# Top-k attention with mixture of depths: half loads ahead of the scores, and the last keys' product in the tiling of the values

## The chip, the cores and the metric

The kernel runs on one core of one Trainium2 chip. The metric is the device time of one execution in microseconds (us). Five engines with queues of their own work beside each other: PE (TensorE, matrix products; its weight loads are listed as PEld), DVE (VectorE), ACT (ScalarE), POOL (GpSimd) and SP (SyncE, which issues most DMAs). Inputs are in HBM, tiles in SBUF (128 partitions), results of PE in PSUM.

## The reference

```python
scores = scale * np.matmul(q, k.transpose(0, 1, 3, 2))      # 8 batches, 8 heads, 576 tokens, 64 wide
kth = np.partition(scores, -top_k, axis=-1)[..., -top_k:-top_k + 1]   # top_k = 32
scores = np.where(scores >= kth, scores, -1000000000.0)
attn = softmax(scores)
x = concat_heads(np.matmul(attn, v))                        # (8, 576, 512)
...
gate = x @ w_gate                                           # per token
top_idx = the 128 tokens of the batch with the largest gate
out = x
out[top_idx] = x[top_idx] + sigmoid(gate) * (relu(x[top_idx] @ w1) @ w2)   # w1 512 x 1024
```

All in float32.

## The kernel before

**Tiles.** The 576 tokens of a batch are 4 tiles of 128 and one of 64 (J = 4, R = 64). A unit is one tile of queries with two heads; for the tile of 64 it holds four heads, two of them on the upper 64 partitions. So a batch has 4 x 4 + 2 = 18 units, and the 8 batches 144. In what follows, "step i" of a batch is the i-th of its 18.

**The pipeline.** One loop (L1094) runs over steps n and has five units in flight. In step n, in the order of the program: the scores of unit n-4 are turned, masked and exponentiated (`weigh`, L1123); the mask of unit n-3 is made (L1126); the scores of unit n+1 are multiplied (`multiply`, L1131); a piece of the next batch's k or q is turned (the half loads, L1135); the values of unit n-4 are multiplied (`values`, L1142); DVE looks for a lower bound of the 32nd largest score of unit n (`bound_of`) and for the 32nd largest itself of unit n-2 (`kth_of`); ACT and POOL prepare unit n-1 for it (`what_is_below`: ACT writes sides, POOL writes y in two halves and a short third instruction). Behind that comes a piece of the MLP of the batch before (`mixtures`, L1179). Every engine's order is that of the program (`InOrder`, L37); only `late`, `vector_late` and `pool_late` hold a few instructions back to fixed places.

**The turned scores on PE.** `turn` (L482) and `turn_last` (L491) make nine pairs: a transpose of 128 x 128 scores (float32, against ident), and a product that adds a large negative number where the mask less is set (bf16). Eight pairs go to the tile ptr, the ninth, with the last 64 keys of both heads, to the upper columns of av. ACT's exponentials then write pT (from ptr) and last (from av).

**The scores on PE.** `multiply` (L355) takes 64 rows of kT and qT (one head's width) by up to 128 queries, so it runs in PE's tiling of 64 rows by 128 columns (64\*128 in the profile). Its result goes to the one buffer of the tile ps, 288 columns in each of four banks. The upper columns of two of the banks are the room for half loads (`halves`, L1134). `keep` (L372) copies the scores to SBUF on ACT (sc).

**The half loads.** `Rows` (L214) fetches k and q of the next batch by rows on SP's queue and turns them to kT and qT: in 16 pieces of two 128 x 128 transposes (`turn`, tiling 128\*128), and two pieces for the last 64 tokens (`turn_last`, 64 rows, tiling 64\*128). When the second piece of a buffer is turned, the next rows are fetched (L283). Each piece is a pair of functions (`parts`, L297): the first turns on PE, the second copies to kT or qT on ACT. `loads_at` (L994) gives one piece to most steps, two to steps 14 and 15; steps 1 and 3 get the pieces of the last 64 tokens, steps 2 and 16 none. In the last batch there are none, and in the first one they begin at step 2.

**The values on PE.** `values` (L503) multiplies pT by v for queries 0 to 63 and 64 to 127 apart, into the lower and upper 64 partitions of av (128 rows by 64 columns, 128\*64). The product of the last 64 keys follows (last by vpair, two heads at once): for a tile of 128 queries one product of 128 queries (128\*128), for the tile of 64 queries two of 64 (128\*64). `keep_values` (L535) copies av to xs on ACT.

The lines of the loop around the change (L1128 to L1142):

```python
        if is_unit(n + 1):
            b, t, g = units[n + 1]
            ps = room_for_scores()
            multiply(t, g, *qkv[b][0:2], ps)
            b, i = divmod(n, per_batch)
            loads = list(islice(loading, first_loads[i] if b == 0 else loads_at[i]))
            halves = [ps[:, a, :, HALF : HALF + P] for a in range(2)]
            for load, half in zip(loads, halves):
                load[0](half)
            scs[n + 1] = keep(ps, n == -1)
            for load, half in zip(loads, halves):
                load[1](half)
```

On DVE, besides the search: prod (`dot`, L940, the gate: x times w_gate, added up), junk (ranks of the gates), pick, low and, in step 0, one half of a mask (less). The float32 product of a transpose or of other operands shows in the profile as several instructions where PE takes more than one pass.

Of the kernel before, what the change touches and what calls it, by code (L numbers as in the profile page):

```python
# [31 lines left out]
J = 4  # L32
# [16 lines left out]
def kernel(  # L49
# [12 lines left out]
    P = nc.NUM_PARTITIONS  # L62
# [6 lines left out]
    R = S - JP  # L69
    HALF = S // 2  # L70
    DE = D + 1
# [96 lines left out]
    def load_weights():  # L168
        sp.dma_start(
            out=wg, in_=dataclasses.replace(moe_w_gate, ap=[[0, P], [1, HD]])  # L170
        )
        sp.dma_start(out=w1, in_=moe_w1.rearrange("(c p) f -> p c f", p=P))
        sp.dma_start(out=w2, in_=moe_w2.rearrange("(c p) n -> p c n", p=P))
# [13 lines left out]
    def flush():  # L187
        while late:
            late.pop(0)()
# [15 lines left out]
    def room_for_qkv(b):  # L205

        kT = kqpool.tile([P, NHP, R + S], FP32, name="kT")  # L210
        qT = kqpool.tile([P, NHP, S], FP32, name="qT")
        return kT, qT, vbufs[b % 2]

    class Rows:  # L214
# [70 lines left out]
        def keep(self, i, tr, c0=0, c1=J, copy=None):  # L285
            copy = copy or act.copy
            if i % 2 == 0:
                to = self.kT[:, i // 2, R + c0 * P : R + c1 * P]
            else:
                to = self.qT[:, i // 2, c0 * P : c1 * P]  # L290
            to = to.rearrange("p (c i) -> p c i", i=P)
            if i % 2 == 0:
                copy(out=to, in_=tr)
            else:
                act.mul(out=to, in_=tr, mul=SMALLER)
# [15 lines left out]
    def turn_pair(rows, hp, copy=None):  # L311
        tr = ps_tr.tile([P, 2, J, P], FP32, name="ptr")
        for w in range(2):
            rows.turn(2 * hp + w, tr[:, w, :, :])
        for w in range(2):
            rows.keep(2 * hp + w, tr[:, w, :, :], copy=copy)
# [8 lines left out]
    def load_v(vb, vs):  # L325
        vt, vpair = vs
        v_rows = vb[:, JP:S, :].rearrange("h p d -> p h d")
        for hh in range(2):
            sp.dma_start(
                out=vpair[hh * R : (hh + 1) * R, :, hh, 0:D], in_=v_rows[:, hh::2, :]  # L330
            )
        for h in range(H):
            sp.dma_start(
                out=vt[:, h, :, 0:D],
                in_=vb[h, 0:JP, :].rearrange("(p j) d -> p j d", j=J),
            )
# [5 lines left out]
    def heads_of(t, g):  # L342

        if t == J:
            return [[(4 * g + i, 0), (4 * g + 2 + i, R)] for i in range(2)]
        return [[(2 * g + i, 0)] for i in range(2)]  # L350

    def room_for_scores():
        return ps_sc.tile([P, 2, 2, 512], FP32, name="ps")

    def multiply(t, g, kT, qT, ps):  # L355

        n = R if t == J else P  # L360
        for u in range(2):
            for i, heads in enumerate(heads_of(t, g)):
                at = u * HALF + (0 if i else R)
                d = slice(i * D, (i + 1) * D)
                for h, r in heads:
                    pe.matmul(
                        ps[r : r + n, i, u, 0:HALF],
                        qT[d, h // 2, t * P : t * P + n],
                        kT[d, h // 2, at : at + HALF],
                    )  # L370
# [106 lines left out]
    def room_to_turn():  # L477
        return ps_tr.tile([P, 2, J, P], FP32, name="ptr"), ps_av.tile(
            [P, 512], FP32, name="av"
        )  # L480
# [22 lines left out]
    def values(t, g, pT, last, av, vs):  # L503

        vt, vpair = vs
        n = R if t == J else P
        for i, heads in enumerate(heads_of(t, g)):
            for c in range(J):
                for r in (0, R):
                    h = heads[-1 if r else 0][0]
                    pe.matmul(
                        av[r : r + R, i * DE : (i + 1) * DE],
                        pT[:, i, c, r : r + R],
                        vt[:, h, c, :],  # L520
                        start=(c == 0 and i == 0),
                        stop=False,
                        skip_group_check=True,
                    )
        for h, r in heads_of(t, g)[0]:
            pe.matmul(
                av[r : r + n, 0 : 2 * DE],
                last[:, r : r + n],
                vpair[:, h // 2, :, :].rearrange("p h e -> p (h e)"),
                start=False,  # L530
                stop=True,
                skip_group_check=True,
            )
# [9 lines left out]
    def normalise(b, t, xs):  # L543
        n = R if t == J else P
        den = sums[0:n, b * NT + t, :]
        divide(n, xs, of_batch[b][0][0:n, t, :], den)
# [407 lines left out]
    def gates(b, t):  # L954
        dot_tile(t, *of_batch[b])
# [51 lines left out]
    for b in range(B - 1):  # L1007
        n = (b + 1) * per_batch + mix_at_of.get(b, mix_at)[6]
# [3 lines left out]
    qkv = {0: room_for_qkv(0)}  # L1012
# [18 lines left out]
    scs, bounds, ys, next8s, masks = {}, {}, {}, {}, {}  # L1031

    def is_unit(n):
        return 0 <= n < N
# [59 lines left out]
    for n in range(-1, N):  # L1094
        b, i = divmod(n, per_batch)
        if i == 0 and 0 <= b < B - 1:
            qkv[b + 1] = room_for_qkv(b + 1)
            loading = chain(
                loading, Rows(k[b + 1], q[b + 1], *qkv[b + 1][0:2]).parts()
            )  # L1100
        if 0 < n + 1 < NHP:
            turn_pair(first_rows, n + 1)
        if n == 1:
            load_v(v[0], qkv[0][2])
        if n == NHP:
            load_weights()


        gating = normalised
        if inverting is not None:  # L1110
            normalised = inverting[0:2]
            vector_late.insert(0, lambda a=inverting: normalise(*a))
            inverting = None
        else:
            normalised = None
        if gating is not None:
            vector_late.append(lambda a=gating: gates(*a))

        if is_unit(n - 4):
            tr, av = room_to_turn()
            pT, last, exp = weigh(scs.pop(n - 4), tr, av, masks.pop(n - 4))  # L1123
            exp()
        if is_unit(n - 3):
            mask_of(n - 3, (act, None) if n in scatter_steps else None)  # L1126
        flush()
        if is_unit(n + 1):  # L1128
            b, t, g = units[n + 1]
            ps = room_for_scores()  # L1130
            multiply(t, g, *qkv[b][0:2], ps)  # L1131
            b, i = divmod(n, per_batch)
            loads = list(islice(loading, first_loads[i] if b == 0 else loads_at[i]))
            halves = [ps[:, a, :, HALF : HALF + P] for a in range(2)]  # L1134
            for load, half in zip(loads, halves):  # L1135
                load[0](half)
            scs[n + 1] = keep(ps, n == -1)
            for load, half in zip(loads, halves):
                load[1](half)
        if is_unit(n - 4):  # L1140
            b4, t4, g4 = units[n - 4]
            values(t4, g4, pT, last, av, qkv[b4][2])  # L1142
            if n in place_steps:
                values_bank[0] = av
                next(mixtures[place_steps[n]])
            if g4 == 0:
                xs = xpool.tile([P, H, DE], FP32, name="xs")
                if t4 == 0:
                    x = xpool.tile([P, NT, HD], FP32, name="x")
                    pg = gates_of[b4 % 2]  # L1150
                    of_batch[b4] = x, pg
            keep_values(t4, g4, av, xs)
            if g4 == groups(t4) - 1:
                inverting = b4, t4, xs
                n4 = R if t4 == J else P
                keep_sums(n4, xs, sums[0:n4, b4 * NT + t4, :])
            while kept:
                kept.pop(0)()


        if is_unit(n):
            bound_of(n)
        flush_vector()
        flush_pool()
        if is_unit(n - 2):
            kth_of(n - 2)
        while after_kth:
            after_kth.pop(0)()


        if is_unit(n - 1):
            what_is_below(n - 1)

        if gating is not None:
            b, t = gating
            if t == J:
                store(out[b], of_batch[b][0])
                mixtures[b] = mixture(float(b * S), of_batch[b][1], ranks[:, b, :])
        for b in mix_steps.get(n, ()):  # L1179
            next(mixtures[b], None)  # L1180
        b, i = divmod(n, per_batch)
        if i == v_at and 0 <= b < B - 1:
            load_v(v[b + 1], qkv[b + 1][2])
# [220 lines left out]
```

## Time and profile before

| | us |
|---|---|
| three runs: median, lowest, highest | 833.55, 833.13, 837.34 |
| the profiled execution | 837.12 |
| its span (first to last instruction) | 834.8 |
| PE busy in the span | 792.3 |
| DVE busy | 795.3 |
| ACT busy | 735.2 |
| POOL busy | 728.4 |

The granted clock of PE is full from 60 us on. In the timeline, a row gives start, duration, engine, operation, out<-in, tiling (PE only), shape and count; in brackets, how long the engine was idle before it and what ended that. PE's products are pipelined, so the distance from start to start is what one costs, not its duration. The table by windows gives the window, its length, and for each engine the busy time in it (and the number of instructions): PE, PEld, DVE, ACT, POOL, then the granted clock, the share of DMA and GB/s. A row of waits reads: who waited, for whom; us in total, times, longest. Where a tile's view is shown, the three numbers behind the count are the shortest, median and longest duration in ns.

### The profile page before, as it was taken

The numbers are of one execution on the slowest core, as the hardware profiler recorded it, in microseconds if no ns is written. First come the engines' busy times: TensorE is split into PE (matmuls) and PEld (weight loads), VectorE is DVE, ScalarE is ACT, GpSimd is POOL, SyncE is SP. The second block draws the span as 40 slices with busy tenths as digits, with TensorE's granted clock in tenths as the row PEclk, the third lists the DMA queues.
The fourth block names the chain that finished last, engine by engine and source line by source line (L and its number), as shares of the span: only waits on it lengthen the run. The fifth ranks groups of instructions, "written<-read, shape, count | busy, mean of one in ns | idle before, by whom it ended". The sixth has DMA issues, their size and how long they took to land. (4 is left out here: it accounts for less than half of the span.)

```text
span 834.8 us, 27764 instructions
## 1 busy us (share of the span) xinstructions
PE 792.3 (95%) x9887; PEld 613.0 (73%) x9887; DVE 795.3 (95%) x4651; ACT 735.2 (88%) x1557; POOL 728.4 (87%) x722
## 2 busy tenths in 40 slices
PE   6899889998999999999999999999999999999977
PEld 5677667766887778777787777877788778867844
DVE  7899999999999999999999999999999999899960
ACT  4799999999999999999999999999999999879831
POOL 4699999999999899999999999999999999989831
PEclk9699999999999999999999999999999999999999
DMA  7931112321151221511233221412215102101011
GB/s 171 284 78 36 32 65 54 78 52 27 59 101 24 53 46 54 111 40 39 78 63 67 48 47 59 98 27 53 40 59 111 27 2 77 23 2 27 3 70 29
DMA packets 122130, 50.35 MB, mean 60 GB/s; under 512 B 116416, under 2 KB 116416, under 8 KB 120960
## 3 DMA queue, kind: packets, MB, share of 16 engines
q1 hardware_dynamic: 118672, 43.91, 22.0%
q0 software_dynamic: 1728, 4.20, 2.7%
q8 instruction: 80, 1.31, 0.7%
q14 instruction: 66, 0.54, 0.3%
q10 hardware_dynamic: 1584, 0.39, 0.2%
HBM read 36.93 MB, written 11.55 MB: 58 GB/s over the span
## 5 line engine op out<-in xcount | busy, mean ns | idle before, releaser
L45 POOL TENSOR_TENSOR y<-sc,sides 128x576 f32<-128x576 f32 x288 | 366.3, 1294 | 65.4 <-ACT sides L45 62.5
L45 DVE MAX8 cand<-sc 128x8 f32<-128x82 f32 (+1 forms) x2016 | 313.8, 227 | 2.2 <-ACT sc L45 2.2
L45 POOL TENSOR_SCALAR less<-sc,next 128x576 bf16<-128x576 f32 x135 | 233.5, 1729 | 2.8 <-DVE next L45 1.9
L45 ACT ACTIVATE sides<-sc,bound 128x576 bf16<-128x576 f32 x288 | 222.0, 780 | 0.0
L45 PE MATMUL ptr<-out_of_reach,less 128*128 128x128 bf16 x1136 | 205.4, 220 | 14.1 <-POOL less L45 13.9
L45 PE MATMUL ptr<-ident,sc 128*128 128x128 f32 x1136 | 215.1, 280 | 0.0
L45 DVE MAX8 next<-y 128x8 f32<-128x584 f32 x288 | 204.5, 752 | 2.8 <-POOL y L45 2.6
L45 PE MATMUL ps<-kT,qT 64*128 64x288 f32 (+1 forms) x1280 | 181.0, 431 | 7.6 <-ACT qT L45 5.8
L45 ACT ACTIVATE pT<-ptr 128x1024 f32<-128x1024 f32 x142 | 145.2, 1022 | 38.6 <-PE ptr L45 34.8
L45 PEld LDWEIGHTS ptr<-ident,sc 128*128 128x128 f32 x1136 | 161.4, 142 | 22.4 <-PE av L45 8.7
L45 PEld LDWEIGHTS av<-v,pT 128*64 128x64 f32 x4544 | 144.1, 137 | 39.4 <-ACT last L45 24.2
L45 PE MATMUL av<-v,pT 128*64 128x65 f32 x4544 | 163.8, 224 | 8.2 <-ACT last L45 8.2
L45 ACT COPY sc<-ps 128x1152 f32<-128x1152 f32 (+1 forms) x144 | 161.1, 1119 | 9.6 <-PE ps L45 9.0
L45 PEld LDWEIGHTS <-less 128*128 128x128 bf16 x1296 | 134.1, 104 | 33.5 <-POOL less L45 19.5
L45 PEld LDWEIGHTS ps<-kT,qT 64*128 64x128 f32 (+1 forms) x1280 | 97.8, 177 | 46.6 <-issue 22.0
L45 ACT ACTIVATE less<-sc,next 128x576 bf16<-128x576 f32 x143 | 111.2, 777 | 6.4 <-DVE next L45 6.0
L45 DVE MATCH_REPLACE8 cand<-best,cand 128x21 f32<-128x21 f32 (+1 forms) x576 | 98.9, 179 | 0.0
L45 DVE MAX8 best<-cand 128x8 f32<-128x21 f32 (+1 forms) x576 | 90.2, 189 | 0.0
L45 PE MATMUL av<-vpair,last 128*128 128x130 f32 (+1 forms) x314 | 68.1, 317 | 0.0
L45 PE MATMUL h_ps<-xeT,w 128*128 128x128 f32 x464 | 61.6, 277 | 0.0
L45 ACT ACTIVATION_READ_ACCUMULATOR sides<-sc,bound 128x1 f32 x288 | 58.0, 201 | 0.0
L45 PEld LDWEIGHTS h_ps<-xeT,w 128*128 128x128 f32 x464 | 56.0, 192 | 2.1 <-issue 1.2
(133 smaller groups left out, 905.8 us busy)
## 6 DMA issues: line engine op xcount, KB each, us to landing
v<-in_v_dram SPq DMA_DIRECT2D x64, 128.0 KB, 3.7
out_dram<-x SPq DMA_DIRECT2D x8, 1024.0 KB, 4.0
rows<-in_k_dram SPq DMA_DIRECT2D x56, 128.0 KB, 3.0
rows<-in_q_dram SPq DMA_DIRECT2D x56, 128.0 KB, 3.0
w<-in_moe_w_dram SPq DMA_DIRECT2D x2, 2048.0 KB
gate_row<-row_dram SPq DMA_DIRECT2D x7, 288.0 KB, 4.5
w<-in_k_dram SPq DMA_DIRECT2D x8, 128.0 KB, 3.2
last<-in_k_dram SPq DMA_DIRECT2D x8, 128.0 KB, 3.6
```

Source lines behind the costliest of these rows:

```text
L45: return lambda *a, **kw: self._tc.keep_in_program_order(fn(*a, **kw))
```

## The change

In a step, the half loads are turned on PE ahead of the scores, and ACT copies them to kT or qT ahead of the copy of the scores. And the product of the last keys is always made as two products of 64 queries.

```diff
@@ values @@
         vt, vpair = vs
-        n = R if t == J else P
         for i, heads in enumerate(heads_of(t, g)):
...
-        for h, r in heads_of(t, g)[0]:
+        for r in (0, R):
+            h = heads_of(t, g)[0][-1 if r else 0][0]
             pe.matmul(
-                av[r : r + n, 0 : 2 * DE],
-                last[:, r : r + n],
+                av[r : r + R, 0 : 2 * DE],
+                last[:, r : r + R],
                 vpair[:, h // 2, :, :].rearrange("p h e -> p (h e)"),
                 start=False,
                 stop=True,
@@ the loop @@
             ps = room_for_scores()
-            multiply(t, g, *qkv[b][0:2], ps)
+            kT, qT = qkv[b][0:2]
             b, i = divmod(n, per_batch)
             loads = list(islice(loading, first_loads[i] if b == 0 else loads_at[i]))
             halves = [ps[:, a, :, HALF : HALF + P] for a in range(2)]
             for load, half in zip(loads, halves):
                 load[0](half)
-            scs[n + 1] = keep(ps, n == -1)
+            multiply(t, g, kT, qT, ps)
             for load, half in zip(loads, halves):
                 load[1](half)
+            scs[n + 1] = keep(ps, n == -1)
```

## Prediction

> **What bounds the kernel now.** I read the busy shares first, then the same for one batch in the middle, then the waits of that part, and last the timeline of single steps; the chain that ended last covers only the closing 0.1% of this span and says nothing here.
>
> ```profile
> PE 792.3 (95%) x9887; PEld 613.0 (73%) x9887; DVE 795.3 (95%) x4651; ACT 735.2 (88%) x1557; POOL 728.4 (87%) x722
> ...
> 418.00:516.00 98.00, 97.00 (x1233) 75.43 (x1231) 97.89 (x576) 92.00 (x198) 90.66 (x87) 1.00 0.27 59
> ...
> ACT pT L45 <- PE ptr L45: 21.7, 58, 0.6
> PE av L45 <- ACT last L45: 4.0, 8, 0.6
> ...
> PE ptr L45 <- POOL less L45: 12.6, 22, 1.2
> ...
> L45 DVE CUSTOM_DVE_ANT_0 prod<-x,wg x40: 672/1128/1752, 57.5 to 804.7; 128x512 f32<-128x512 f32 x32, 64x512 f32<-64x512 f32 x8
> ```
>
> The second line is the batch from 418 to 516 us: PE is busy for 97.00 of 98 us and DVE for 97.89. Both look like the bound, and the change touches only PE and the order on ACT, so everything hangs on which of the two it is. The next two lines are from 220 to 690 us: in 58 steps the exponential of the turned scores (pT) starts when PE has finished, and PE itself waits 8 times, 4.0 us. The line on POOL less is from 60 to 780 us; from 220 us on it is gone, so those 22 waits of PE lie early, and there PE is not the bound. The last line says why DVE's 97.89 is not a fixed amount of work: the same instruction prod takes 0.67 to 1.75 us.
>
> ```profile
> 442.17 2.52 POOL L45 TENSOR_TENSOR y<-sc,sides 128x576 f32<-128x576 f32 x2
> 443.15 1.02 ACT L45 ACTIVATE pT<-ptr 128x1024 f32<-128x1024 f32 x1 [0.37 <-PE ptr L45]
> 443.22 1.24 PE L45 MATMUL ps<-kT,qT 64*128 64x288 f32 x8
> 444.04 1.20 DVE L45 CUSTOM_DVE_ANT_0 prod<-x,wg 128x512 f32<-128x512 f32 x1
> 444.39 0.44 PE L45 MATMUL ps<-ident,rows 128*128 128x128 f32 x2
> 444.76 1.16 PE L45 MATMUL av<-v,pT 128*64 128x65 f32 x32
> 445.84 0.49 PE L45 MATMUL av<-vpair,last 128*128 128x130 f32 x2
> 446.17 1.05 PE L45 MATMUL h_ps<-xeT,w 128*128 128x128 f32 x8
> ```
>
> This is one step. On PE it goes, start to start: turned scores 441.58 to 443.22 (1.64 us), scores 1.17, half load 0.37, values 1.08, last keys 0.33, MLP product 0.89; the sum, 5.48, is the distance of this pT (443.15) from the next (448.64). PE works through without a gap and ACT waits 0.37 us for it: PE sets the pace. DVE's prod starts at 444.04, while POOL's two y run to 444.69, and ends 0.55 us after them: of its 1.20 us some 0.53 are standing behind POOL. From 225 to 690 us the prod (24, mean 1199 ns, least 672), less (4, 1213 against 501), pick (5, 582 against 286) and low (4, 377 against 174) stand like this for 12.6 + 2.8 + 1.5 + 0.8 = 17.7 us, 3.7 us in a batch. POOL's y wait for ACT's sides, ACT for PE. So DVE is full, but part of its time is a wait whose end PE sets.
>
> In each batch of 18 steps this holds from step 4 to the pT of step 0 of the next batch. In between ACT paces five steps (pT from 492.78 to 519.35, 5.31 us each, no wait), and PE's waits for "last" lie there (0.57 and 0.43 us); a faster PE only waits longer there.
>
> **Edit 1, half loads before the scores.** At every switch of PE's tiling the next weights are not loaded early: the weight loads stand idle for 0.16 us ahead of the scores, 0.39 ahead of the half load and 0.17 ahead of the values (440 to 446 us). Before, a step with a half load of 128 rows goes 128\*128, 64\*128 (scores), 128\*128 (half load), 128\*64 (values). After, the half load joins the turned scores, and one excursion is gone. The same step without a half load is in the last batch:
>
> ```profile
> 710.48 0.22 PE L45 MATMUL av<-out_of_reach,less 128*128 128x128 bf16 x1
> 710.62 1.24 PE L45 MATMUL ps<-kT,qT 64*128 64x288 f32 x8
> 711.81 1.15 PE L45 MATMUL av<-v,pT 128*64 128x65 f32 x32
> ```
>
> Before, from the last less product of the turned scores to the values: 0.15 + 1.17 + 0.37 = 1.69 us. After: less to the first transpose 0.06 (as inside the turned scores), transpose to transpose 0.11 (the four of xe follow each other so: 500.73 to 501.17), the last transpose to the next tiling 0.20 (0.20 from the half load's second transpose to the values, at 444.56 and 444.76), scores to values 1.19 (710.62 to 711.81). Sum 1.56 us. At the trace's full resolution the two sums are 1.689 and 1.548: **0.14 us saved in a step**. What the trace lacks is the switch from this transpose to the scores' tiling; nearest are that 0.20 and the 0.15 from a bf16 product to the scores. With 0.15 the saving is 0.19. At the dear end the gap after the scores, 0.33 us, is put there too, and the saving is 0.01. I take 0.20: it is from the same kind of instruction. With two half loads in a step the saving is the same, since their extra transposes cost 0.11 us in either place. The loads of the last 64 tokens (64 rows, the scores' own tiling) had no switch before (scores 1.07 us); they may gain one and cost up to 0.1 us, but both lie in the ACT-paced steps 1 and 3, where PE has its 0.57 and 0.43 us of wait for cover.
>
> **How many steps.** Half loads of 128 rows lie in steps 0, 4 to 15 and 17. Of these, 13 are in the PE-paced run of a batch (4 to 15 and 17). Such runs are whole in batches 3 to 6; in batch 2 it starts at step 6 (11 steps); batches 0 and 1 are paced by POOL, ACT and DVE (the 22 waits for less), and the last batch loads nothing. 11 + 4 x 13 = 63 steps x 0.14 = **8.8 us**.
>
> **The order on ACT.** The copy of the half load (0.38 us, 0.55 for two) goes ahead of the copy of the scores. Nothing is added, and xs and sides come after both as before. The half load's copy now waits for the scores, as the scores' copy before waited for the half load; that end comes earlier by 0.15 us. The scores are ready for DVE 0.4 to 0.55 us later. In batches 3 to 6 they lie ready 1.7 to 3.5 us before their first MAX8, so that is hidden. It isn't in the start: DVE waits for the scores at 24.96 (1.37 us) and at 36.01 (0.79 us), and there it costs 0.2 to 0.3 us each. I set **0.5 us**; the end for no cover at all is 98 steps (14 in each of 7 batches) x 0.39 = 38 us, which would need DVE to wait for sc, and after 60 us it never does. The scores' buffer is released at the same time, since the two copies end together. The turns also fetch the next rows on SP's queue: their order there is the same, each fetch some 1.2 us earlier, and rows land 3 us after the issue but are used two steps, 11 us, later; PE has no wait for them now.
>
> **Edit 2, the last keys in the values' tiling.** Steps that hold the last tokens do it like this already:
>
> ```profile
> 412.78 0.39 PE L45 MATMUL av<-vpair,last 128*64 128x130 f32 x4
> 413.11 1.16 PE L45 MATMUL h_ps<-xeT,w 128*128 128x128 f32 x8
> 414.10 0.27 PE L45 MATMUL ptr<-ident,sc 128*128 128x128 f32 x1
> ```
>
> Values, last keys and MLP product: before 1.08 + 0.33 + 0.89 = 2.30 us. In the other form 0.98 + 0.33 + 0.99 = 2.30 us. The switch only moves behind the product: **0 us**, with ends of 0.05 us either way in a step (3 us in 63). The result in av is ready 0.1 us or more earlier for xs, which ACT almost never waits for.
>
> **What is late next.** When POOL's y come earlier by what PE saves, DVE stands shorter behind them. Within a run PE leads by 0.14 us more each step; prod of step 9 (0.53 us over its least time), 13 (0.81), 17 (0.93) and less in step 0 (0.72) take that up one after the other. To follow, DVE has to give up 8.8 of its 17.7 us. It then has less than half of its reserve left, and the masks on ACT come 0.65 us or more after the kth value that they read. I take 0.3 us off for places where DVE does not follow.
>
> The Trainium skill speaks against this. Its page "Perfetto Trace Analysis", section "Identifying the Most-Contended Engine", names the engine with the highest occupancy as the one to work on, and for the tensor engine it takes the share of weight loads, not of products. By that DVE with 97.89 of 98 us is the bound and PE with 75.43 us of loads is not, and the sum would be 0. The case's row for prod, 0.67 to 1.75 us for the same shape, is what I go by.
>
> **Sum.** 8.8 - 0.5 - 0.3 = 8.0 us less. The profiled execution took 837.12 us, 2.3 more than its span of 834.8, and stands 3.6 us above the median of 833.55; it would be 829.1 us. The median goes to **825.5 us**.
>
> **Rivals.**
> - DVE is the bound after all (0 to 2 us gained, 831.5 to 835.5, middle 833.3): its gap is 0.1 us in a batch. For it: when DVE ran late (160 to 225 us), ACT's masks waited for it. Against: DVE's own least time in a batch is 97.9 - 3.7 = 94.2 us, less than the 96.3 us which the batch would take.
> - Half of the gain (828.5 to 831.5): the switch after the transpose costs near its dear end, or DVE follows only in the later half of each run.
> - Slower: a DVE instruction that shares with POOL now arrives just after the first y of a pair has ended and stands behind the whole second one, 1.26 us. The place is low, which arrives 0.3 us ahead of that border in steps 2 of batches 3 to 7, and then one prod more per batch. It decides once POOL leads DVE by more than 0.3 us at step 2. Price: 2 x 1.26 x 5 = 12.6 us, less the 8.0 gained if PE's saving still counted, so +4.6: 838.2 us. Against: a DVE that is late stands shorter at its next place.
> - The order isn't as written: excluded; in the changed program's order on PE the half loads stand between the turned scores and the scores.
>
> **Chances.** Forecast, 822 to 828.5: 0.60. Half: 0.14. No gain: 0.17. Slower, 836 to 842: 0.07. More than the sum (switch at its cheap end, 0.19 x 63 = 12 us, 821): 0.02. A measurement can tell about 0.5% here, 4.2 us: the border 829.4 leaves the forecast, the last case and 0.06 of the half case on the faster side, 0.68; 0.25 same; 0.07 slower. The range 821.5 to 834.0 leaves out the slower case and the upper part of no gain.
>
> **What would show it.** Right: the pT distance of PE-paced steps falls from 5.48 to 5.34 us, the half load stands before the scores at 0.2 us, scores to values 1.19 us; a batch takes 96.2 to 96.5 us for 98; DVE stays full and the mean of prod falls from 1.2 towards 0.9 us. Wrong: PE gets waits for less, ACT's less for next, and a batch still takes 98 us (the first rival); prod or low longer than before (the slower one); a gap over 0.3 us between half load and scores (the half case).

## The result

The changed kernel takes 826.26 us (median of 5 runs, 825.69 to 828.44) against 835.58 for the kernel before in the same measurement (5 runs, 833.13 to 837.34). The ratio is 0.9898, with a 95% interval from 0.9879 to 0.9918: by the ratio some 8.5 us less (the two medians lie 9.3 us apart). The forecast was 8.0 us less, and a median of 825.5 us. The profiled execution took 828.44 us (829.1 forecast), and its span is 826.1 us for 834.8.

Where the 8.7 us of the span went is read from the starts of pT in the steps 0, batch by batch:

| from pT of step 0 of a batch to that of the next | before | after | less |
|---|---|---|---|
| up to the first pT and batch 0 | 104.58 | 103.88 | 0.70 |
| batch 1 | 93.47 | 94.04 | -0.57 |
| batch 2 | 98.55 | 96.54 | 2.01 |
| batch 3 | 98.08 | 96.21 | 1.87 |
| batch 4 | 98.09 | 96.11 | 1.98 |
| batch 5 | 98.08 | 96.10 | 1.98 |
| batch 6 | 98.11 | 96.11 | 2.00 |
| last batch | 100.30 | 101.30 | -1.00 |
| the rest, to the end of the span | 45.53 | 45.81 | -0.28 |

The gain lies in batches 2 to 6, 9.84 us in all, and the last batch gives 1.0 us of it back. At the start the executions of all kernels here differ by more than these two do: the first pT came at 30.2 to 32.4 us, and batch 0 took 71.8 to 73.0 us from there, with no order among the kernels. Batch 1 took 94.04 to 94.08 us in the changed kernel and in the five others that have its order on PE and no product of 128 queries for the last keys, and 93.47 to 93.95 us in the other eight. So at least a part of the loss in batch 1 seems to belong to the two edits together; no run here shows why.

### The profile page after: what moved, and what is told of

Same layout as the page of the kernel before. It is cut to its first block, busy times and chain, and to the rows that moved or that the text cites. A ratio compares the mean times of both kernels' runs of the same rounds, so it can differ in the third digit from the quotient of the medians.

```text
span 826.1 us, 28252 instructions
## 1 busy us (share of the span) xinstructions
PE 777.0 (94%) x10143; PEld 596.5 (72%) x10143; DVE 787.2 (95%) x4651; ACT 730.7 (88%) x1557; POOL 715.4 (87%) x722
## 3 DMA queue, kind: packets, MB, share of 16 engines
q8 instruction: 82, 1.34, 0.8%
## 5 line engine op out<-in xcount | busy, mean ns | idle before, releaser
L45 PE MATMUL ptr<-out_of_reach,less 128*128 128x128 bf16 x1136 | 205.3, 220 | 19.5 <-POOL less L45 19.4
L45 PEld LDWEIGHTS <-less 128*128 128x128 bf16 x1296 | 136.1, 106 | 39.2 <-POOL less L45 25.2
L45 PEld LDWEIGHTS ps<-kT,qT 64*128 64x128 f32 (+1 forms) x1280 | 100.2, 178 | 41.5 <-issue 21.2
L45 PE MATMUL h_ps<-xeT,w 128*128 128x128 f32 x464 | 65.8, 286 | 0.0
L45 PE MATMUL y_ps<-w,hT 128*128 128x512 f32 x112 | 60.6, 636 | 0.0
L45 ACT ACTIVATION_READ_ACCUMULATOR sides<-sc,bound 128x1 f32 x288 | 59.9, 208 | 0.0
```

The lines of the kernel that those rows point to most:

```text
L45: return lambda *a, **kw: self._tc.keep_in_program_order(fn(*a, **kw))
```

## The profile after

The same views as before the change, of the changed kernel. First the busy shares:

```profile
PE 777.0 (94%) x10143; PEld 596.5 (72%) x10143; DVE 787.2 (95%) x4651; ACT 730.7 (88%) x1557; POOL 715.4 (87%) x722
```

Then one batch in the middle, by windows (window, length, busy time of PE, PEld, DVE, ACT, POOL):

```profile
410.00:506.10 96.10, 94.93 (x1263) 73.58 (x1262) 95.99 (x579) 91.49 (x197) 88.55 (x88) 1.00 0.27 60
```

PE lost 2.1 us of busy time in a batch, and DVE 1.9, though it does the same work: it is as full as before, 95.99 of 96.10 us. A DVE that is full at 98 us and full again at 96 was not full of work. Where its 2 us were is seen in its groups from 225 to 690 us (count, then busy us and mean ns):

```profile
L45 DVE CUSTOM_DVE_ANT_0 prod<-x,wg 128x512 f32<-128x512 f32 x19 | 16.9, 887 | 0.0
L45 DVE CUSTOM_DVE_ANT_0 prod<-x,wg 64x512 f32<-64x512 f32 x5 | 4.9, 985 | 0.0
L45 DVE TENSOR_SCALAR low<-bound 128x36 int32<-128x36 int32 x4 | 4.2, 1061 | 0.0
L45 DVE TENSOR_SCALAR less<-sc,next 128x576 bf16<-128x576 f32 x5 | 2.5, 504 | 0.0
L45 DVE TENSOR_SCALAR pick<-slot,ranks 128x128 bf16<-128x128 f32 x5 | 1.4, 287 | 0.3
```

The 24 prod fell from a mean of 1199 to 907 ns (24 x 292 = 7.0 us), less from 1213 to 504, pick from 582 to 287. But low rose, from 377 to 1061 ns. The waits of the changed kernel from 220 to 690 us:

```profile
ACT pT L45 <- PE ptr L45: 19.4, 54, 0.6
...
POOL less L45 <- DVE next L45: 6.8, 18, 0.6
...
PE av L45 <- ACT last L45: 4.7, 9, 0.7
```

PE still ends 54 waits of the exponential (58 before). New is the line in the middle: POOL now waits 18 times for DVE's kth values, which it did once before in this part (0.4 us). And one step by the timeline, the neighbour of the one that the prediction shows:

```profile
438.53 0.39 PE L45 MATMUL ps<-ident,rows 128*128 128x128 f32 x2
438.56 1.02 ACT L45 ACTIVATE pT<-ptr 128x1024 f32<-128x1024 f32 x1 [0.24 <-PE ptr L45]
438.84 1.24 PE L45 MATMUL ps<-kT,qT 64*128 64x288 f32 x8
440.01 1.15 PE L45 MATMUL av<-v,pT 128*64 128x65 f32 x32
440.39 1.71 POOL L45 TENSOR_SCALAR less<-sc,next 128x576 bf16<-128x576 f32 x1
440.78 0.89 DVE L45 CUSTOM_DVE_ANT_0 prod<-x,wg 128x512 f32<-128x512 f32 x1
441.00 0.39 PE L45 MATMUL av<-vpair,last 128*64 128x130 f32 x4
441.32 1.16 PE L45 MATMUL h_ps<-xeT,w 128*128 128x128 f32 x8
```

From start to start on PE: half load 0.32 us, scores 1.17, values 0.98, last keys 0.32, MLP product 0.99, and the turned scores that follow 1.54. The sum is 5.33, as is the distance to the next pT (443.89). The half load's second transpose starts 0.20 us before the scores, and the turned scores cost 0.10 less since the half load follows them in the same tiling. On DVE, prod now starts inside POOL's less and no longer inside y.

Taken step by step, the distance of pT fell by 0.14 to 0.15 us in each of steps 5 to 15 of batches 3 to 6, also where it was not 5.48 (5.44 to 5.30 with a product for y_ps, 5.66 to 5.52 with two half loads).

## The experiments

The theory: PE sets the pace in the larger part of batches 2 to 6, and the saved change of tiling is worth 0.14 us in such a step and nothing in another. The rivals: the gain is from another part of the change (ACT's order, the last keys), or it is spread over all steps, or DVE was the bound and was helped in some indirect way. "Batch" is below the distance of pT from step 0 to step 0, in batches 3 to 6.

| kernel | us | ratio to before | batch, us | last batch, us |
|---|---|---|---|---|
| before | 835.58 | 1 | 98.1 | 100.3 |
| changed | 826.26 | 0.9898 [0.9879, 0.9918] | 96.1 to 96.2 | 101.3 |
| loads_first_only | 827.06 | 0.9903 [0.9886, 0.992] | 96.2 | 100.8 |
| pe_order_only | 825.5 | 0.9885 [0.9865, 0.9905] | 96.1 to 96.2 | 101.3 |
| split_last_only | 835.27 | 0.9993 [0.998, 1.0005] | 98.1 | 100.4 |
| act_order_only | 836.0 | 1.0007 [0.9998, 1.0016] | 98.0 | 100.5 |
| loads_first_uncounted | 835.98 | 0.9989 [0.9978, 1.0] | 98.0 | 100.2 |
| before_without_low | 836.49 | 0.9996 [0.9985, 1.0008] | 98.0 to 98.3 | 100.1 |
| after_without_low | 826.49 | 0.988 [0.9859, 0.99] | 96.0 to 96.3 | 100.05 |
| before_without_last_keys | 825.24 | 0.9863 [0.9842, 0.9883] | 96.0 | 101.0 |
| after_without_last_keys | 826.28 | 0.9872 [0.9852, 0.9891] | 96.0 | 101.4 |
| after_without_both | 824.32 | 0.984 [0.9818, 0.9862] | 95.5 | 99.1 |
| low_behind_kth | 826.6 | 0.988 [0.9859, 0.9901] | 96.0 | 100.3 |
| parts_that_pay | 827.11 | 0.9893 [0.9875, 0.9911] | 96.1 | 100.55 |

The ratios are each against the kernel before as it ran beside them (its median was 835.7 to 837.1 us), so the times of different groups of runs are compared by their ratios.

### Which part of the change

Edit 1 alone (loads_first_only is the changed kernel with the old product of the last keys):

> Edit 1 alone: half loads ahead of the scores on PE and ACT, the last keys' product as before. Theory (the excursion of PE's tiling that is gone, 0.14 us in each PE-paced step): the whole gain, 0.988 to 0.992 of before, and a PE-paced step of 5.34 us. Rival (the last keys' product gives a good part): under half of it, 0.995 or more.

Edit 2 alone (split_last_only is the kernel before with the diff's part in `values`):

> Edit 2 alone: the last keys' product as two of 64 queries, half loads behind the scores as before. Theory: the switch only moves behind the product, so 0.998 to 1.002 of before and a step of 5.48 us. Rival (this edit gives a good part): 0.995 or less.

The changed kernel with ACT's old order (pe_order_only):

```diff
             multiply(t, g, kT, qT, ps)
+            scs[n + 1] = keep(ps, n == -1)
             for load, half in zip(loads, halves):
                 load[1](half)
-            scs[n + 1] = keep(ps, n == -1)
```

> The changed kernel, but ACT copies the scores ahead of the half loads as before; PE's order is the changed one. Theory (PE's tiling): the same as the changed kernel, 0.988 to 0.992 of before, or up to 0.001 less, since DVE gets the scores 0.4 us earlier. Rival (the new order on ACT moves POOL and DVE against each other, and that is the gain): 0.997 or more.

And the kernel before with ACT's new order only (act_order_only, `keep` moved behind the loop of load[1], PE's order as before):

> The kernel before, but ACT copies the half loads ahead of the scores; PE's order is that of before. Theory (PE's tiling): 0.999 to 1.002 of before, a step of 5.48 us, perhaps 0.5 us more at the start. Rival (ACT's order is the gain): 0.992 or less.

Measured: 0.9903 for edit 1 and 0.9993 for edit 2; ACT's order by itself 1.0007, and taking it out of the changed kernel leaves 0.9885, inside the interval of the change. So the order on PE alone carries the gain, and both other parts are worth nothing that can be told from the times.

### Which steps count

The scores go behind the half loads only in the steps that the prediction did not count (loads_first_uncounted, from the kernel before):

```diff
+            first = b < 2 or i < 4
+            if not first:
+                multiply(t, g, kT, qT, ps)
...
             for load, half in zip(loads, halves):
                 load[0](half)
+            if first:
+                multiply(t, g, kT, qT, ps)
```

> The kernel before, with the scores behind the half loads on PE only where PE does not set the pace: everywhere in batches 0 and 1 and in steps 0 to 3 of the others (33 of the 98 steps with a half load of 128 rows or 64 rows). Theory (only the 0.14 to 0.15 us of a PE-paced step counts): no change, 0.999 to 1.001 of before (835.7 us), batches 3 to 6 still 98.1 us. Rival (the gain is spread over all steps with a half load, or it comes from the start and the ends): 33/98 of the 9.4 us, some 3 us, 0.996.

0.9989, with an interval from 0.9978 to 1.0: a third of the moved loads, and at most 0.2% of time. The rival's 0.996 is outside. One batch of this kernel by windows, and its waits from 220 to 690 us:

```profile
393.79:491.84 98.05, 96.97 (x1232) 75.43 (x1230) 97.94 (x577) 92.03 (x197) 90.70 (x88) 1.00 0.27 59
```

```profile
ACT pT L45 <- PE ptr L45: 23.0, 60, 0.6
```

It is the kernel before again: 98.05 us a batch and 60 waits for PE. A step gains only where PE sets the pace.

### Was DVE the bound, and is it now

The four instructions of `keep_least` on DVE left out in batches 0 to 6, from the kernel before and from the changed one (this leaves out part of a check on the bounds; least is preset to 1):

```diff
         if i == per_batch - 1 and b < B - 1:
-            keep_least(b, bounds.pop(b)[:, :, :, 7], next8s.pop(b)[:, :, :, 7])
+            bounds.pop(b), next8s.pop(b)
```

> The kernel before without the instruction low and the three small ones behind it on DVE, in batches 0 to 6 (the check that the search's bounds were low enough is left out there). DVE loses about 0.45 us of work a batch and the waiting of low behind POOL. Theory (PE sets the pace, DVE's fullness is waiting): 0 to -0.3 us a batch, 0.998 to 1.001 in all. Rival (DVE is the bound of the kernel before): -0.45 to -0.6 us a batch, 3 to 4 us in all, 0.995 to 0.996.

> The changed kernel, with the same cut (the check of the bounds left out in batches 0 to 6). There low takes 1.06 us in place of 0.17 at its least, since it stands behind POOL's second y. If PE still sets the pace in batches 2 to 6: under 0.3 us a batch, 825 to 827 us. If DVE has become the bound with it: 0.45 us of work and up to 0.9 us of waiting a batch, 820 to 823 us.

Before, the cut gives 0.9996: DVE with 97.9 of 98 us busy was not the bound. The four instructions overlap; from the start of low to that of the instruction behind the four it is 0.44 us in step 2 of batch 1, where low doesn't stand, and 0.59 to 0.67 us in the steps 2 of batches 3 to 7. All of it can go without effect, and DVE stays as full without it (97.92 of 98.03 us in a batch), since its prod stand longer: 1318 ns on average for 1199, from 225 to 690 us. In the changed kernel three of the four batches take 96.0 us and one 96.3, for 96.1 to 96.2, though there the four took DVE 1.28 to 1.34 us. PE still ends 57 waits of pT from 220 to 690 us (54 with low), so there, too, PE sets the pace.

Now the other side, PE relieved. The product of the last 64 keys is left out (the values of these keys are missing from the result), in the changed kernel:

```diff
-        for r in (0, R):
-            h = heads_of(t, g)[0][-1 if r else 0][0]
-            pe.matmul(
-                av[r : r + R, 0 : 2 * DE],
...
-            )
```

> The changed kernel without the product of the last 64 keys on PE (the values of those keys are left out of the result). It takes 0.32 us a step from start to start, of which some 0.2 to 0.3 us go from a PE-paced step. If PE alone sets the pace: 65 steps by 0.2 us, 13 us less, 813 us, and batches of 93.5 us. If DVE follows only down to its own least time (94.2 us a batch by its shortest instructions, batches now 96.1): at most 1.9 us a batch, and more likely 0.3 to 1, 820 to 825 us.

It brings nothing that can be told from the times (826.28 us, 0.9872), and batches of 96.0 us for 96.1. I had expected 0.3 to 1 us a batch from it. Its waits from 220 to 690 us:

```profile
ACT less L45 <- DVE next L45: 16.6, 35, 0.6
...
PE av L45 <- ACT last L45: 12.5, 24, 0.8
...
ACT pT L45 <- PE ptr L45: 2.9, 11, 0.3
```

Compared with the changed kernel, the waits of pT for PE fell from 19.4 to 2.9 us, and in their place ACT waits 35 times for DVE's kth values. PE is no longer the one that comes last. So 0.1 us below the changed kernel's batch another limit stands, and DVE is in the waits that show it.

If that is so, the kernel before should come to the same 96.0 us by any relief of PE, whatever its kind. The same cut, from the kernel before with its order unchanged:

> The kernel before, its order unchanged, without the product of the last 64 keys on PE (the values of those keys are left out of the result). It takes some 0.33 us of a step of 5.48 us. Theory (before, PE sets the pace, and 0.1 us below the changed kernel's 96.1 us a batch stands a floor that DVE sets): batches 3 to 6 fall from 98.1 to 96.0 us, no further, and the time to 825 to 828 us, about what the change brings in another way. Rival 1 (PE alone sets the pace, no floor): 13 times 0.2 to 0.33 us a batch, 93.8 to 95.5 us, 812 to 822 us. Rival 2 (DVE was the bound of the kernel before and the change helped it in some other way than by PE's time): 98 us, no change.

Measured: 0.9863, batches of 95.97 to 95.99 us. The product of the last keys costs 0.33 us a step there, and 13 x 0.33 would be 4.3 us a batch; it got 2.1. Of these 2.1 us the change takes 1.98, so it brings nearly all that PE alone can bring in this kernel, as far as this cut shows.

Both cuts together, in the changed kernel:

> The changed kernel without the product of the last keys on PE (their values are left out) and without low and the three small instructions behind it on DVE in batches 0 to 6 (a check on the bounds is left out). Each cut alone left a batch at 96.0 us. Theory (PE and DVE both stand at 96.0 us, so that only both cuts together move it): DVE loses 0.9 us of standing and 0.7 to 0.8 us of work a batch, so batches of 94.3 to 95.3 us and 815 to 822 us. Rival (a third thing, ACT with its 5.31 us a step, holds 96.0): batches of 95.6 to 96.0 us, 824 to 827 us.

Here my theory missed: 0.984, and batches of 95.53 us, below the 96.0 of each cut alone, but not the 94.3 to 95.3 that I had worked out (with 0.7 to 0.8 us for the work of the four instructions, which overlap and are 0.44). One batch of it by windows, and waits in that window:

```profile
389.37:484.90 95.53, 92.49 (x1192) 71.43 (x1191) 95.11 (x575) 91.00 (x197) 89.17 (x88) 1.00 0.29 60
```

```profile
ACT less L45 <- DVE next L45: 2.6, 6, 0.6
POOL less L45 <- DVE next L45: 1.5, 3, 0.8
...
ACT pT L45 <- PE ptr L45: 1.4, 4, 0.6
```

DVE now has 0.4 us to spare and ACT waits both for DVE and for PE. The rival's number (95.6, ACT's 5.31 us a step) is nearer than mine, but an ACT that waits 4.0 us in a batch is not the bound by itself. The two cuts show that PE and a second limit stand within 0.1 us of each other at 96.0, and that DVE is part of the second: leaving the same work out on DVE brings 0.5 us a batch once PE is relieved, and 0.1 us while it isn't. What holds the batch at 95.5 stays open: the loop through DVE's bound, ACT's sides, POOL's y and DVE's kth value is my guess, and no run here shows it.

### The place of low

In the changed kernel low arrives on DVE just after POOL's second y has begun. Before (timeline; the group of two y is 1.26 us each):

```profile
502.81 2.53 POOL L45 TENSOR_TENSOR y<-sc,sides 128x576 f32<-128x576 f32 x2 [0.84 <-ACT sides L45]
503.75 0.39 DVE L45 TENSOR_SCALAR low<-bound 128x36 int32<-128x36 int32 x1
```

After:

```profile
496.82 2.52 POOL L45 TENSOR_TENSOR y<-sc,sides 128x576 f32<-128x576 f32 x2 [0.85 <-ACT sides L45]
498.33 1.06 DVE L45 TENSOR_SCALAR low<-bound 128x36 int32<-128x36 int32 x1
```

It came 0.94 us after the first y began, and it ended with it; now it comes 1.51 us after, and stands until the second y is over (499.34). In low_behind_kth it is moved to another place of the step:

```diff
-            keep_least(b, bounds.pop(b)[:, :, :, 7], next8s.pop(b)[:, :, :, 7])
+            of = bounds.pop(b)[:, :, :, 7], next8s.pop(b)[:, :, :, 7]
+            after_kth.append(lambda: keep_least(b, *of))
```

> The changed kernel with all its work, and low with the three small instructions behind it moved on DVE from ahead of the search for a bound to behind the search for the 32nd largest, where POOL makes less and not y. Theory (low's 0.9 us behind the second y costs little while PE sets the pace, but a full us in the last batch, where PE has no half loads): batches of 96.0 to 96.1 us, the last one 100.1 to 100.4 in place of 101.3 us, 1 to 2 us less than the changed kernel: 0.986 to 0.989 of before. Rival (low's wait costs nothing anywhere, or its new place costs as much): the last batch stays at 101.3 us, 0.990.

The group of low from 225 to 690 us (shortest, median, longest in ns):

```profile
L45 DVE TENSOR_SCALAR low<-bound x4: 362/374/376, 309.1 to 597.2; 128x36 int32<-128x36 int32 x4
```

It is back at its old length, a batch takes 96.0 us for 96.1, the last batch is back at 100.3 us, and the ratio is 0.988. Lastly PE's order and this place, and nothing else of the change (parts_that_pay):

> The kernel before with the half loads ahead of the scores on PE only (ACT's order and the last keys' product as before), and low with its three small instructions behind the search for the 32nd largest on DVE. Theory (what pays is PE's order, and low's new place is worth some 2 us more, 1.0 of them in the last batch): batches 3 to 6 of 96.0 us, the last one of 100.1 to 100.4 us, and a profiled execution about 2 us shorter from batch 2 to the end than the changed kernel's; 0.986 to 0.9885 of before. Rival (the 1.84 us of the last run were chance, or belong to ACT's order): a last batch of over 101 us, 0.9885 to 0.991.

0.9893, with a last batch of 100.55 us and batches of 96.1. The theory missed: from batch 2 to the end its profiled execution is 0.7 us shorter than the changed kernel's (627.5 for 628.2 us), not 2, and the ratio lies in the rival's range. By the profiles, most of the 1 us of the last batch comes back; in the times, neither version can be told from the changed kernel (0.9859 to 0.9911 against 0.9879 to 0.9918). No version here beats it by what can be measured.

### Where the last batch loses its 1.0 us

All but 0.14 of it lies in one step, 9: from one pT to the next it takes 7.30 us for 6.44. Before (timeline; DVE's last ranks, and ACT's mask):

```profile
737.80 0.81 DVE L45 TENSOR_SCALAR_CACHE_REDUCE junk<-gate_row,gate 64x576 f32<-64x576 f32 x1
738.70 1.02 ACT L45 ACTIVATE pT<-ptr 128x1024 f32<-128x1024 f32 x1 [0.76 <-PE ptr L45]
741.71 0.78 ACT L45 ACTIVATE less<-sc,next 128x576 bf16<-128x576 f32 x1 [1.82 <-DVE next L45]
```

After:

```profile
728.83 0.80 DVE L45 TENSOR_SCALAR_CACHE_REDUCE junk<-gate_row,gate 64x576 f32<-64x576 f32 x1
728.87 1.02 ACT L45 ACTIVATE pT<-ptr 128x1024 f32<-128x1024 f32 x1
732.75 0.78 ACT L45 ACTIVATE less<-sc,next 128x576 bf16<-128x576 f32 x1 [2.68 <-DVE next L45]
```

DVE's ranks begin 0.90 us before pT in the kernel before and 0.04 before it in the changed one: DVE comes into the last batch 0.86 us later against ACT. In this step, where it has three ranks to make, ACT waits for it in both kernels, 1.82 and 2.68 us. The debt that PE's pace hides in the batches ahead is paid here. With low left out the step takes 6.23 us, with low moved 6.45 (low_behind_kth) and 6.69 (parts_that_pay), so low is a good part of the debt. It isn't all of it: in loads_first_only low stands as long (1.09 us in the last batch, 1.01 in the changed kernel), and the step takes 6.92 us.

## Why the prediction was right, point by point

- **The bound.** Right. "PE sets the pace" is what before_without_low (no effect) and before_without_last_keys (2.1 us a batch) show from both sides. The Trainium skill's rule in "Perfetto Trace Analysis", section "Identifying the Most-Contended Engine" would have put the change at 0. The runs speak against it for the kernel before, and for it one step later: at 96.0 us a batch, DVE's fullness has become one of the limits.
- **0.14 us in a step.** Right: 5.48 to 5.33 or 5.34 us. The switch from the half load's transpose to the scores, which the trace of before did not have, takes 0.20 us (92 times from 60 us on, all 0.202 or 0.203), the one I took; the ends of 0.15 and 0.33 did not come. Scores to values was put at 1.19 and is 1.17.
- **63 steps, 8.8 us.** Mis-sized: batches 2 to 6 gained 9.84 us. In batch 2 the paced run starts at step 5, not 6, and its gain is 2.01 us where 11 steps were to give 1.54. In the others it is 1.98 on average for 1.82. Steps 5 to 15 give what was forecast. Step 4 was counted too, though the five steps that the prediction gives to ACT (492.78 to 519.35 us) are the steps 0 to 4; steps 3 and 4 together gained 0.03 us, and 0.10 in low_behind_kth, where low doesn't stand behind the second y. Steps 16 and 17 gained 0.39 us together where one saving of 0.14 was counted. The 0.09 of step 16 belong to the last keys (0.09 in split_last_only, 0.00 in loads_first_only). The 0.30 of step 17 belong to PE's order (0.30 in loads_first_only): half of it is the forecast saving, and the other half came with a wait that is gone, of the pT that ends this step for the ninth pair in av (ACT pT for PE av from 220 to 690 us: 5 times, 3.0 us before; once, 0.2 us after). Why that wait went isn't shown. So the 1.98 us for 1.82 are not a better saving in each step; gains that nobody had counted made up for step 4.
- **The start, 0.5 us.** Not seen. The part up to batch 2 became 0.13 us shorter, act_order_only and pe_order_only put ACT's order within the interval of nothing, and the spread between executions at the start is larger than the term. Batch 1 is 94.1 us in pe_order_only as well, so its loss is not from ACT's order.
- **0.3 us where DVE does not follow.** Mis-sized and misplaced: in the paced runs DVE follows, and the last batch costs 1.0 us, with what lies behind it 1.28 (of which 0.28 is within the spread there: that part took 45.3 to 46.3 us in all kernels but after_without_both). 9.84 + 0.13 - 1.28 = 8.69 us in all; that the forecast's 8.0 came out so near is partly luck, since its terms were off in opposite ways.
- **The last keys, 0 us.** Right: 0.9993.
- **What is late next.** Half right. DVE was to give up 8.8 of its 17.7 us of standing behind POOL; it gave up 7.0 (prod) + 2.8 (four less) + 1.5 (five pick) - 2.7 (four low) = 8.6 us. Low does what the slower rival said, at the place it named: it stands behind the whole second y. The rival's price did not come: it added 0.68 us a batch to low, not 1.26, no prod grew with it, and while PE is the one that comes last it cost 0.1 us a batch (96.1 for the 96.0 of low_behind_kth, in steps 3 and 4). What failed is the step "it then has less than half of its reserve left". By the shortest durations DVE needs 94.2 us a batch, and I took the difference to 96.1 for reserve. The runs with less on PE show a floor at 96.0: the rest of the standing (0.9 us in low, 1.1 in five prod) does not go when PE gets faster still. The forecast stopped 0.1 us short of a limit that it did not see; with the cheap end of the switch (0.19 us a step) it would have been too hopeful.

## What to carry to other kernels

- An engine at 99.9% busy is the bound only if its busy time is work: compare the durations of the same instruction, and leave out a piece of its work to see. Here 0.6 us a batch could go from the full engine with no effect, and 0.14 us a step from PE moved the kernel by 1%.
- Order the groups on PE so that products of one tiling stand together; count the saving only in steps where PE comes last.
- Before costing a second step of the same kind, make the engine much faster by leaving work out: the cut that took 4.3 us a batch off PE and brought 2.1 tells how far the next limit is away.

## What the runs showed of the hardware beyond that

- **POOL's less holds prod only at its start.** All 24 prod of the changed kernel from 225 to 690 us start 0.17 to 0.63 us after a less on POOL. One that starts 0.63 us after it takes its shortest 0.67 us; at 0.39 it takes 0.89 and at 0.17 1.11, so each ends some 1.28 us after the less began, while the less goes on to 1.72. Before, 22 of the 24 started inside y, and one that came 0.22 us after the beginning of the second y took 1.60 us and ended 0.55 us after it. Of the other two, one started 0.08 us after a less and took its shortest 0.67 us, and there the less took 2.26 us: the less stood. The Trainium skill, "SBUF — State Buffer", section "Who interferes with whom", says that a DVE instruction with two SBUF inputs contends with a GpSimd instruction that reads SBUF, through ports which they share under an exclusive lock; that the lock lasts for the whole instruction it says of DVE's 2-port modes. Held against a lock for the whole of POOL's instruction, the rows of y agree to 0.12 us (prod ends 0.55 us after y for a shortest 0.67); those of less don't, they show 0.6 of 1.72 us. So DVE lost little when it came later against POOL: prod slid from y into less.
- **What a change of tiling costs on PE.** From the start of the last product of one group to the start of the first of the next it is 0.15 us after a bf16 product of the turned scores, 0.20 after a transpose or after the last keys, 0.33 after the scores. That holds the product itself: where the next group has the same tiling, it is 0.06, 0.11 and 0.24 us. So the change adds 0.09 to 0.10 us in each case. The second product behind it comes later as well: the half load's second transpose 0.165 us after the first for 0.115 without a change, the second product of h_ps 0.214 for 0.112. For the half load that is 0.10 + 0.05 us, the 0.14 to 0.15 by which a step got shorter.
